# Softmax attention beside a gated FFN: key tiles in blocks of three and two instead of steps of two, a fifth score bank, one accumulator, and the FFN's matmul pairs spread by a planned table

## The chip, the cores and the metric

One core of a Trainium2 chip runs the whole program. The metric is the device time of one execution in microseconds (us). Three executions of the kernel before took 1433.26 to 1434.07 us, 1433.64 us in the median. One further execution was profiled. Its trace has the time of each instruction on TensorE (PE, with its weight loads as PEld), VectorE (DVE), ScalarE (ACT), GpSimd (POOL) and the DMA queues.

## What is computed

The inputs are x of 2048 tokens by 512, the attention weights, and the FFN's three weights with an inner width of 1792. The attention has 32 heads of 16.

```python
def _A_ref(x, wqkv, wo):
    H = 32; Dh = D // H
    qkv = (lambda x, *d: x.transpose(*d))((x @ wqkv).reshape(B, S, 3, H, Dh), 2, 0, 3, 1, 4)
    q, k, v = qkv[0], qkv[1], qkv[2]
    scale = Dh ** -0.5
    scores = jnp.einsum("bhqd,bhkd->bhqk", q, k) * scale
    p = _softmax(scores, axis=-1)
    o = jnp.einsum("bhqk,bhkd->bhqd", p, v)
    return (lambda x, *d: x.transpose(*d))(o, 0, 2, 1, 3).reshape(B, S, D) @ wo

def _B_ref(x, w_gate, w_up, w_down):
    g = _silu(x @ w_gate)
    u = x @ w_up
    return (g * u) @ w_down

x = A_x
xn = _layernorm(x, axis=-1)
s = _A_ref(xn, A_wqkv, A_wo)
g = _silu(_B_ref(xn, B_w_gate, B_w_up, B_w_down))
return x + s * g
```

## The kernel before

A prologue of some 157 us makes the layer norm, the projections to queries, keys and values, and the first FFN tile. Queries and keys go through memory as high and low parts, so that a score matmul has 50 rows (NROW): three products of parts with 16 rows each, and two rows for a shift.

Then one long loop holds the attention. It runs over 32 units: 8 groups of four heads by 4 blocks of 512 queries. A unit goes over 16 key tiles of 128 keys, two tiles to a step (kp), so 8 steps a unit and 256 in all. For a key tile there are two pairs of score matmuls (L826), one pair for each j. The two matmuls of a pair work side by side on the upper and lower half of the array's rows and write the two banks of score[j]. ScalarE then makes one exponential over both banks, 128x1024, into a buffer pr (L828). The value matmuls of a step (L357) are issued one step later, by values(prev) after the next step's first key tile. The four heads stand side by side in the array's columns and add into a bank acc[u % 2]. The trace shows each of them as two matmuls, so that a key tile has two groups of four. When a unit is through, finish, called from the list after one step later, lets VectorE transpose acc[u % 2], divide by the sums and store.

Between the attention's matmuls stand those of the FFN, and at the end those of the output projection. They come as pairs (L175): a matmul into bankx from the upper half of the rows, one into banky from the lower half. ffn and project_out are generators that yield after each pair, and fill(n) takes the next n pairs. A gate and up tile has 24 pairs. When its last pair is issued, ScalarE makes a tanh from bankx (L204), and VectorE multiplies, then splits the result into hh and the down weights into wd (L167, L168, L145, L146). A down tile has 24 or 18 pairs, and its sum is added into facc or y on VectorE. share() calls fill once a step, after the step's four score pairs, with the next number of shares: a gate tile in three steps of 8, a down tile in two or three, an output tile in one step of 12. FIRST sets how many pairs stand between the score pairs of the first step.

The order on each engine is as the program is written (the schedule is manual). ScalarE and VectorE take their instructions in that order. PSUM's eight banks are four for the scores, bankx, banky, and two for acc. Keys and values of a group of heads lie in rings of five chunks of four tiles (RING), loaded by SyncE's queue; queries in two buffers.

Of the kernel before, what the change touches and what calls it, by code (L numbers as in the profile page):

```python
# [19 lines left out]
P = 128  # L20
# [26 lines left out]
KSLOT = (0, 0, 1)  # L47


@with_exitstack  # L50
def tile_block(ctx: ExitStack, tc: tile.TileContext, x, wqkv, wo, w_gate, w_up, w_down, out):
# [24 lines left out]
    banks = (bankx, banky)  # L76
    acc = [pone.tile([P, 512], F32, name=f"acc{i}") for i in range(2)]
    fx = one.tile([P, 2, DC, TB], F32R, name="fx")
# [272 lines left out]
    def values(item):  # L351
        u, kp, probs = item
        v, a = vst[(u // NB * NB + kp * 2 // CT) % RING], acc[u % 2]
        for i in range(2):
            kt = 2 * kp + i
            for h in range(4):
                mm(a[h * 32:h * 32 + DH + 1], v[:, kt % CT, h * (DH + 1):(h + 1) * (DH + 1)],  # L357
                   probs[2 * i + h // 2][:, h % 2], start=kt == 0, stop=kt == KT - 1, skip_group_check=True)

    def normalise(u, first, last, between=None):  # L360
        g, b = divmod(u, NB)
        n = last - first
        o1 = late.tile([P, TB], F32, tag="o1", name="o1")
        dve.transpose(o1[:, :n], acc[u % 2][:, first:last])
        ov = o1[:, :n].rearrange("p (c d) -> p c d", d=32)
        rl = late.tile([P, TB // 32], F32, tag="rl", name="rl")[:, :n // 32]
        dve.reciprocal(rl, ov[:, :, DH])
        if between:
            between()
        dst = on[b][:, first:last].rearrange("p (c s d) -> p c s d", s=2, d=DH)[:, :, g % 2]  # L370
        dve.tensor_mul(dst, ov[:, :, :DH], rl[:, :, None].to_broadcast([P, n // 32, DH]))

    def finish(u):
        g, b = divmod(u, NB)
        normalise(u, 0, TB)
        if g % 2:
            o2 = late.tile([P, TB], F32, tag="o2", name="o2")
# [11 lines left out]
    steps = KT // 2  # L389

# [20 lines left out]

    shares = []

    def plan():
        def tile_of(n, parts):
            shares.extend([n // parts] * parts)

        halved = 0  # L420
        for i in range(2 * NB):
            nf = GROUPS[i % 2].stop - GROUPS[i % 2].start
            for f in range(nf - (i == 0)):
                tile_of(3 * DC, 3 if i or f else 2)
            for t in range(NT):
                if nf == FG:
                    halved += HALVED
                    tile_of(3 * nf, 3 - halved // (NB * NT))
                    halved %= NB * NT
                else:  # L430
                    tile_of(3 * nf, 2)
        for _ in range(EARLY):
            tile_of(3 * (DT - 1), 1)
        for _ in range(NB * NT - NT):
            tile_of(3 * DT, 1)
        shares[0] += 2 - sum(FIRST[:3])
        shares[1] -= 2 + FIRST[3]

    def blocked():
        return not queue or queue[0][0] is not None and ready[queue[0][0]] < DT  # L440

    def share():
        if not blocked() and shares:
            fill(shares.pop(0))


    with ExitStack() as pro:
# [3 lines left out]
        p5 = pro.enter_context(tc.tile_pool(name="p5", bufs=2))  # L451
        plast = pro.enter_context(tc.tile_pool(name="plast", bufs=1))
        pps = pro.enter_context(tc.tile_pool(name="pps", bufs=4, space=PSUM))

        xin = facc
# [48 lines left out]
        for _ in range(11):  # L504
            mm(acc[1][:, :P], busy, busy, start=True, stop=True)
        for kind, i in ((load_w, 8), (load_tile, 1), (load_w, 9), (load_w, 10), (load_tile, 2), (load_w, 11),
# [56 lines left out]
        def turn(t):  # L563
            for c in range(DT):
                turn_one(acc[t % 2], t, c)
            return acc[t % 2].rearrange("p (c f) -> p c f", f=P)

# [41 lines left out]
        xf = one.tile([P, DT, P], F32, tag="th", name="xf")  # L609
        for c, to in enumerate((acc[0], bankx, acc[1], banky)):  # L610
            turn_one(to, 0, c)
        for c, to in enumerate((acc[0], bankx, acc[1], banky)):
            if c == 2:
# [39 lines left out]
        def value_tile(b, t):  # L653
# [9 lines left out]
            else:  # L663
                ps = project([(vh[:, c], vl[:, c], c) for c in range(DT)], xh, xl, slice(t * P, (t + 1) * P), order,
                             acc[1] if b == t == NB - 1 else None)
            if b == 0 and t == 1:
# [16 lines left out]
        for b in range(NB):  # L683
# [3 lines left out]
            for n, (make, i) in enumerate(slots):  # L687
# [12 lines left out]
                if not more and n == 2:  # L700
                    split_gu(0)
                    for bank in acc:
                        dve.memset(bank, 0.0)
                if not more and n in (1, 3):
# [51 lines left out]
        with tc.If(fast < 1):  # L756
            with tc.tile_pool(name="gen", bufs=1) as gen:
                for h in range(2):
                    pool.memset(qst[0][h * HALF:h * HALF + 2].bitcast(F32), 0.0)
                for g in range(NG):  # L760
                    for b in range(NB):
# [14 lines left out]
                        dve.tensor_scalar(mn, mn, -1.0, None, op0=ALU.mult)  # L776
                        top = acc[0][:4 * NT, :P]
                        nc.tensor.transpose(top, mn, ident)
# [28 lines left out]
    split_hidden()  # L807
    plan()
    prev = None

    exps = []
    for u in range(units):
        g, b = divmod(u, NB)
        q = qst[u % 2]
        for kp in range(steps):
            now = u * steps + kp
            probs = []
            for i in range(2):
                kt = 2 * kp + i
                k, kc = kst[(g * NB + kt // CT) % RING], kt % CT  # L820
                if now == i == 0:
                    fill(FIRST[0])
                for j in range(2):
                    for h in range(2):
                        r = slice(h * HALF, h * HALF + NROW)
                        mm(score[j][:, h], k[r, j, kc * P:(kc + 1) * P], q[r, j], start=True, stop=True)  # L826
                    pr = ppool.tile([P, 2, TB], F32, tag="pr", name="pr")
                    exps.append(act(pr, score[j], AF.Exp, scale=0.25))  # L828
# [32 lines left out]
    lo = one.tile([P, D], F32R, tag="th", name="rl")  # L861
    outs = (score[0][:, 0], score[1][:, 0], acc[units % 2], banky)
    half = TB // 2
    cols = [slice(n * half, (n + 1) * half) for n in range(2)]
    spare, *y = [ppool.tile([P, 2, TB], F32, tag="pr", name="y") for _ in range(3)]
    y = [i[:, n] for i in y for n in range(2)]
# [25 lines left out]
    for n in range(2):  # L892
        normalise(units - 1, n * half, (n + 1) * half, partial(low, 0) if n else None)
        turned.append(spare[:, n])
        dve.transpose(turned[n][:, :half], on[NB - 1][:, cols[n]])
# [39 lines left out]
```

## Time and profile before

| | before |
|---|---|
| profiled execution | 1433.38 us |
| its span in the trace | 1431.3 us |
| granted TensorE clock | 1.0 |
| ScalarE, exponentials | 993.1 us in 1024 instructions |
| VectorE busy | 541.9 us |
| DMA | 149.12 MB, mean 104 GB/s |

A row of the timeline gives the start in us, the duration in us, the engine, the line, the instruction with output and inputs, and how many such instructions are merged in the row. A bracket behind it says how long the engine had been idle and what released it. A row of the groups gives busy time and the mean duration in ns of one, then the idle time before them and what ended it. TensorE's matmuls overlap: durations of one (0.39 us for a matmul of a pair) are longer than the distance from one start to the next, and the distance is what a matmul costs in a stream.

### The profile page before, as it was taken

The page shows a single profiled execution, that of the slowest core. Times are in us where ns is not written, and L with a number is a line of the kernel's source. Part 1 is how long each engine was busy: PE and PEld are TensorE (multiplying, and loading weights), DVE is VectorE, ACT ScalarE, POOL GpSimd, SP SyncE. Part 2 cuts the span into 40 slices and gives each one's busy share as a digit, 9 for nine tenths or more (in the row PEclk, how much of TensorE's full clock was granted, in tenths as well). Part 3 has the DMA queues.
Part 4 walks back from the last instruction along what each step waited for, and adds up shares of the span by engine and source line. Part 5 has one row for each costly group of instructions (what it writes and reads, how often), then busy time and mean ns, then how long its engine had stood idle before and what let it go on. Part 6 is the DMA issues. An engine that isn't in the chain of part 4 may idle for free.

```text
span 1431.3 us, 26760 instructions
## 1 busy us (share of the span) xinstructions
PE 1424.6 (100%) x11197; PEld 801.5 (56%) x11197; DVE 541.9 (38%) x901; ACT 1110.0 (78%) x1235; POOL 91.8 (6%) x104
## 2 busy tenths in 40 slices
PE   9999999999999999999999999999999999999998
PEld 7787655555555555555555555555555555555555
DVE  6544443213523443133324341234243422243665
ACT  6733588888888888788888888888888887888764
POOL 4200100000000000000000000000000000000154
PEclk9999999999999999999999999999999999999999
DMA  7878542142264330143543310342724210412552
GB/s 244 262 244 273 136 101 64 24 98 56 71 146 128 84 78 21 40 104 81 111 124 91 96 48 10 79 109 63 168 79 127 59 43 12 101 31 79 196 184 104
DMA packets 127643, 149.12 MB, mean 104 GB/s; under 512 B 12577, under 2 KB 79649, under 8 KB 126750
## 3 DMA queue, kind: packets, MB, share of 16 engines
q1 hardware_dynamic: 122206, 126.72, 34.8%
q0 software_dynamic: 4880, 20.12, 3.8%
q8 instruction: 89, 1.46, 0.5%
q10 hardware_dynamic: 432, 0.52, 0.1%
q14 instruction: 36, 0.29, 0.1%
HBM read 107.46 MB, written 40.11 MB: 103 GB/s over the span
## 4 chain that ended last, share of the span: by engine, by line
PE 89%; DVE 0%; DVEq 0%; issue 0%
PE acc L357 33%; PE bankx L175 32%; PE score L826 20%; PE banky L175 3%; PE acc L873 0%; PE banky L873 0%; PE score L873 0%; DVE y L880 0%; DVE y L886 0%; DVEq L931 0%
## 5 line engine op out<-in xcount | busy, mean ns | idle before, releaser
L828 ACT ACTIVATE pr<-score 128x1024 f32<-128x1024 f32 x1024 | 993.1, 1023 | 222.9 <-PE score L826 222.2
L357 PE MATMUL acc<-pr,vst 128*17 128x512 f32 x4096 | 489.2, 595 | 0.0
L826 PE MATMUL score<-qst,kst 50*128 50x512 f32 x2048 | 352.0, 421 | 0.0
L826 PEld LDWEIGHTS score<-qst,kst 50*128 50x128 f32 x2048 | 177.0, 184 | 263.8 <-ACT pr L828 225.8
L175 PE MATMUL bankx<-fx,guh 64*128 64x512 f32 x896 | 288.6, 392 | 0.1
L175 PE MATMUL banky<-fx,guh 64*128 64x512 f32 x896 | 288.6, 392 | 0.0
L357 PEld LDWEIGHTS acc<-pr,vst 128*17 128x17 f32 x4096 | 93.9, 96 | 234.4 <-issue 233.6
L205 DVE SCALAR_TENSOR_TENSOR ga<-th,bankx 128x512 f32<-128x512 f32 x56 | 38.5, 688 | 450.3 <-ACT th L204 450.3
L175 PEld LDWEIGHTS bankx<-fx,guh 64*128 64x128 f32 x896 | 165.7, 185 | 34.5 <-DVEq L756 0.6
L175 PE MATMUL bankx<-fx,gul 64*128 64x512 f32 x448 | 175.4, 391 | 0.0
L175 PE MATMUL banky<-fx,gul 64*128 64x512 f32 x448 | 175.4, 391 | 0.0
L175 PEld LDWEIGHTS banky<-fx,guh 64*128 64x128 f32 x896 | 165.7, 185 | 2.8
L175 PE MATMUL banky<-wd,hh 64*128 64x512 f32 x672 | 166.8, 389 | 0.0
L175 PE MATMUL bankx<-wd,hh 64*128 64x512 f32 x672 | 166.8, 389 | 0.0
L175 PEld LDWEIGHTS bankx<-wd,hh 64*128 64x128 f32 x672 | 124.0, 185 | 27.2
L175 PEld LDWEIGHTS banky<-wd,hh 64*128 64x128 f32 x672 | 124.0, 185 | 0.7
L175 PEld LDWEIGHTS bankx<-fx,gul 64*128 64x128 f32 x448 | 82.9, 185 | 17.7
L175 PEld LDWEIGHTS banky<-fx,gul 64*128 64x128 f32 x448 | 82.8, 185 | 1.6
L593 PE MATMUL ps<-xt,wh 128*128 128x512 f32 x256 | 80.9, 396 | 0.1
L223 DVE COPY facc<-bankx 128x512 f32<-128x512 f32 x16 | 11.1, 692 | 171.5 <-PE banky L175 171.5
L136 DVE TENSOR_TENSOR gul<-gur,guh 128x1024 fp32r<-128x1024 f32 x56 | 68.6, 1225 | 2.1
L380 POOL DMA_DIRECT2D o_d<-o x12 | 6.5, 542 | 757.2 <-DVE o L378 757.2
(160 smaller groups left out, 1063.5 us busy)
## 6 DMA issues: line engine op xcount, KB each, us to landing
gur<-in_B_w_gate_dram SPq DMA_DIRECT2D x56, 256.0 KB
gur<-in_B_w_up_dram SPq DMA_DIRECT2D x56, 256.0 KB
wdr<-in_B_w_down_dram SPq DMA_DIRECT2D x56, 256.0 KB
kst<-k_d SPq DMA_DIRECT2D x192, 64.0 KB
qst<-q_d SPq DMA_DIRECT2D x192, 64.0 KB
fx<-xt_d SPq DMA_DIRECT2D x24, 512.0 KB
q_d<-parts SPq DMA_DIRECT2D x16, 512.0 KB
k_d<-parts SPq DMA_DIRECT2D x16, 512.0 KB
```

What stands on the lines that cost most here:

```text
L136: dve.tensor_sub(lo, raw, hi.bitcast(F32))
L175: mm(bank, lhs[h], rhs[h], start=start, stop=stop)
L205: dve.scalar_tensor_tensor(ga, th, 1.0, bankx, op0=ALU.add, op1=ALU.mult)
L223: dve.tensor_copy(facc[:, t], bankx)
L357: mm(a[h * 32:h * 32 + DH + 1], v[:, kt % CT, h * (DH + 1):(h + 1) * (DH + 1)], probs[2 * i + h // 2][:, h % 2], start=kt == 0, stop=kt == ...
L380: (pool if g < NG - 1 else sp).dma_start(o_d[g // 2, b], o2)
L593: mm(ps, w, a[:, c], start=n == 0, stop=n == 3 * DT - 1)
L826: mm(score[j][:, h], k[r, j, kc * P:(kc + 1) * P], q[r, j], start=True, stop=True)
L828: exps.append(act(pr, score[j], AF.Exp, scale=0.25))
```

## The change

A unit's 16 key tiles are now taken in six blocks, four of three tiles and two of two (SIZES), so there are 192 blocks instead of 256 steps. The block's first two score pairs, those of its first tile, stand together as before; then come the values of the block before, and finish where that block ended a unit. The other score pairs stand alone, and after each of them fill takes a share of the FFN's pairs: four shares in a block of three, two in a block of two.

The block's last score pair writes its second matmul into a bank of its own, spare, and its exponential is made as two of 128x512, one from score[1] and one from spare. The bank for this comes from the accumulator, which is now one bank, acc, for all units. The exponentials have eight buffers instead of six. The rings have four chunks instead of five, and the next group's keys and values are loaded when the last unit of a group has done with the values of a chunk.

plan() chooses before the program is built, by dynamic programming over the FFN's tiles, in which order each unit's blocks of three and two stand and how many pairs each block takes. It aims at four pairs to a tile of keys, with at least 12 in a block of three and 6 in a block of two, and no block crosses an FFN tile's border. What it chose:

| key tiles in the block | FFN pairs in the block | blocks | pairs behind the last score pair |
|---|---|---|---|
| 3 | 12 | 94 | 3 |
| 3 | 14 | 1 | 3 |
| 3 | 16 | 31 | 4 |
| 3 | 9 | 2 | 2 |
| 2 | 6 | 17 | 3 |
| 2 | 8 | 43 | 4 |
| 2 | 12 | 4 | 6 |

Units 7 and 8, as an example: (2, 6) (3, 12) (2, 6) (3, 12) (3, 12) (3, 12), then (3, 12) (3, 12) (3, 12) (2, 8) (3, 16) (2, 8).

TensorE's order before, early in the loop, around one step's value matmuls. The names are those of the code; x8 merges the eight value matmuls of two key tiles, and 17x512 is the shape of one output.

```order
L175 MATMUL bankx<-fx,guh 128x512
L175 MATMUL banky<-fx,guh 128x512
L826 MATMUL score_8961<-qst_8975,kst_8963 128x512 x2
L826 MATMUL score_8962<-qst_8975,kst_8963 128x512 x2
L357 MATMUL acc_87<-pr,vst_8964 17x512 x8
L826 MATMUL score_8961<-qst_8975,kst_8963 128x512 x2
L826 MATMUL score_8962<-qst_8975,kst_8963 128x512 x2
L175 MATMUL bankx<-fx,guh 128x512
L175 MATMUL banky<-fx,guh 128x512
L175 MATMUL bankx<-fx,gul 128x512
L175 MATMUL banky<-fx,gul 128x512
```

The same place in the changed program, a block of three after a block of three:

```order
L871 MATMUL score_8965<-qst_8975,kst_548 128x512 x2
L871 MATMUL score_8966<-qst_8975,kst_548 128x512 x2
L416 MATMUL acc<-pr,vst_549 17x512 x12
L871 MATMUL score_8965<-qst_8975,kst_552 128x512 x2
L235 MATMUL bankx<-fx,guh 128x512
L235 MATMUL banky<-fx,guh 128x512
L235 MATMUL bankx<-fx,guh 128x512
L235 MATMUL banky<-fx,guh 128x512
L235 MATMUL bankx<-fx,gul 128x512
L235 MATMUL banky<-fx,gul 128x512
L871 MATMUL score_8966<-qst_8975,kst_552 128x512 x2
L235 MATMUL bankx<-fx,guh 128x512
```

The value matmuls come twelve at a time instead of eight, and the second tile's two score pairs, which stood together, now have three FFN pairs between them. The end of that block on TensorE:

```order
L235 MATMUL banky<-fx,guh 128x512
L235 MATMUL bankx<-fx,gul 128x512
L235 MATMUL banky<-fx,gul 128x512
L871 MATMUL score_8966<-qst_8975,kst_552 128x512
L871 MATMUL spare<-qst_8975,kst_552 128x512
L235 MATMUL bankx<-fx,guh 128x512
L235 MATMUL banky<-fx,guh 128x512
L235 MATMUL bankx<-fx,guh 128x512
L235 MATMUL banky<-fx,guh 128x512
```

The last score pair's second matmul goes to spare. On ScalarE, two steps before (the tanh of a gate tile stands among the exponentials):

```order
L828 ACTIVATE pr<-score_8961 128x1024
L828 ACTIVATE pr<-score_8962 128x1024
L828 ACTIVATE pr<-score_8961 128x1024
L828 ACTIVATE pr<-score_8962 128x1024
L204 ACTIVATE th<-bankx 128x512
L828 ACTIVATE pr<-score_8961 128x1024
L828 ACTIVATE pr<-score_8962 128x1024
L828 ACTIVATE pr<-score_8961 128x1024
L828 ACTIVATE pr<-score_8962 128x1024
```

and the changed program, a block of two and the beginning of the next:

```order
L264 ACTIVATE th<-bankx 128x512
L874 ACTIVATE pr<-score_8965 128x1024
L874 ACTIVATE pr<-score_8966 128x1024
L874 ACTIVATE pr<-score_8965 128x1024
L876 ACTIVATE pr<-score_8966 128x512
L877 ACTIVATE pr<-spare 128x512
L874 ACTIVATE pr<-score_8965 128x1024
L874 ACTIVATE pr<-score_8966 128x1024
```

The block's last exponential has become two halves, and the gate's tanh stands behind a block's halves.

The core of the diff (most of plan, the renamed banks of the prologue and of the tail left out):

```diff
-RING = NB + 1
+RING = NB
...
-FIRST = (4, 5, 2, 2)
-HALVED = 2
+SIZES = {2: 2, 3: 4}
+FIRST = (4, 0, 4, 3, 3, 2, 2)
...
+    least, most = {2: 6, 3: 12}, {2: 12, 3: 16}
...
+                        c = cost + 100 * max(0, least[k] - n) + abs(n - 4 * k)
...
+    for k, n in blocks:
+        m = 2 * k - 2
+        parts.append((k, [0, 0] + [n // m + (i < n % m) for i in range(m)]))
+    parts[0] = 3, list(FIRST[1:])
+    return parts
...
-        u, kp, probs = item
-        v, a = vst[(u // NB * NB + kp * 2 // CT) % RING], acc[u % 2]
-        for i in range(2):
-            kt = 2 * kp + i
+        u, tiles, probs = item
+        for i, kt in enumerate(tiles):
+            v = vst[(u // NB * NB + kt // CT) % RING]
             for h in range(4):
-                mm(a[h * 32:h * 32 + DH + 1], v[:, kt % CT, h * (DH + 1):(h + 1) * (DH + 1)],
+                mm(acc[h * 32:h * 32 + DH + 1], v[:, kt % CT, h * (DH + 1):(h + 1) * (DH + 1)],
                    probs[2 * i + h // 2][:, h % 2], start=kt == 0, stop=kt == KT - 1, skip_group_check=True)
...
-        dve.transpose(o1[:, :n], acc[u % 2][:, first:last])
+        dve.transpose(o1[:, :n], acc[:, first:last])
...
-    ppool = ctx.enter_context(tc.tile_pool(name="ppool", bufs=6))
+    ppool = ctx.enter_context(tc.tile_pool(name="ppool", bufs=8))
...
+    spare = spool.tile([P, 512], F32, name="spare")
...
-        for kp in range(steps):
-            now = u * steps + kp
+        kt = 0
+        for i in range(steps):
+            now = u * steps + i
+            size, parts = blocks[now]
+            tiles = range(kt, kt + size)
+            kt += size
             probs = []
-            for i in range(2):
-                kt = 2 * kp + i
-                k, kc = kst[(g * NB + kt // CT) % RING], kt % CT
-                if now == i == 0:
-                    fill(FIRST[0])
-                for j in range(2):
-                    for h in range(2):
-                        r = slice(h * HALF, h * HALF + NROW)
-                        mm(score[j][:, h], k[r, j, kc * P:(kc + 1) * P], q[r, j], start=True, stop=True)
-                    pr = ppool.tile([P, 2, TB], F32, tag="pr", name="pr")
-                    exps.append(act(pr, score[j], AF.Exp, scale=0.25))
-                    if i == 0 and j == 1 and now:
-                        tc.add_manual_dep(exps[-1].ins, exps[-3].ins.name, settled, reason="order of the slots' writes")
-                    probs.append(pr)
-                    if now == i == 0 and j:
-                        fill(FIRST[1])
-                    elif (now, i, j) in ((0, 1, 0), (1, 0, 0)):
-                        fill(FIRST[2 + now])
-                if i == 0:
+            if not now:
+                fill(FIRST[0])
+            for n in range(2 * size):
+                t, j = tiles[n // 2], n % 2
+                if n == 2:
                     catch_up()
-                if i == 0 and prev:
-                    values(prev)
-            old, prev = prev, (u, kp, probs)
-            share()
-            if old and old[1] == steps - 1:
-                after.append(partial(finish, old[0]))
-            if kp == 0:
-                if u + 1 < units:
-                    load_q(u + 1)
-                    load_shift(u + 1)
-            if g + 1 < NG and (b == 0 and kp == 0 or b == NB - 1 and kp in (2, 4, 6)):
-                load_k(g + 1, kp // 2)
-                load_v(g + 1, kp // 2)
+                    if prev:
+                        values(prev)
+                        if prev[1][-1] == KT - 1:
+                            finish(prev[0])
+                k, kc = kst[(g * NB + t // CT) % RING], t % CT
+
+                room, whole = score[j], n < 2 * size - 1
+                for h in range(2):
+                    r = slice(h * HALF, h * HALF + NROW)
+                    mm(room[:, h] if whole or not h else spare, k[r, j, kc * P:(kc + 1) * P], q[r, j], start=True, stop=True)
+                pr = ppool.tile([P, 2, TB], F32, tag="pr", name="pr")
+                if whole:
+                    made = act(pr, room, AF.Exp, scale=0.25)
+                else:
+                    act(pr[:, 0], room[:, 0], AF.Exp, scale=0.25)
+                    made = act(pr[:, 1], spare, AF.Exp, scale=0.25)
+                exps.append(made)
+                if n == 1 and now:
+                    tc.add_manual_dep(exps[-1].ins, exps[-3].ins.name, settled, reason="order of the slots' writes")
+                probs.append(pr)
+                fill(parts[n])
+            if prev and prev[0] // NB + 1 < NG and prev[0] % NB == NB - 1:
+                done = prev[1][-1] + 1
+                while len(coming) < done // CT:
+                    load_k(prev[0] // NB + 1, len(coming))
+                    load_v(prev[0] // NB + 1, len(coming))
+                    coming.append(now)
+                if done == KT:
+                    coming.clear()
+            prev = u, tiles, probs
+            if i == 0 and u + 1 < units:
+                load_q(u + 1)
+                load_shift(u + 1)
```

More of the change, by code (lines that the diff above doesn't have):

```diff
@@ L47, with plan @@
 KSLOT = (0, 0, 1)
+def plan():
+    sizes = sorted(SIZES)
+    least, most = {2: 6, 3: 12}, {2: 12, 3: 16}
+    left = []
+    for i in range(2 * NB):
+        nf = GROUPS[i % 2].stop - GROUPS[i % 2].start
+        left += [3 * DC] * nf + [3 * nf] * NT
+    left = left[2:]
+    blocks = [(3, sum(FIRST)), (2, 3 * DC - sum(FIRST))]
+    rest = [3 * (DT - 1)] * EARLY + [3 * DT] * (NT * (NB - 1))
+    ends = H // 4 * NB * sum(SIZES.values()) - len(rest)
+    whole = tuple(SIZES[k] for k in sizes)
+    start = tuple(SIZES[k] - sum(b[0] == k for b in blocks) for k in sizes)
+    layers = [{(0, left[0], start): (0, None)}]
+    for _ in range(len(blocks), ends):
+        new = {}
+        for state, (cost, _) in layers[-1].items():
+            tile_no, rem, kinds = state
+            kinds = kinds if any(kinds) else whole
+            for i, k in enumerate(sizes):
+                if not kinds[i]:
+                    continue
+                for n in range(least[2] // 2, min(most[k], rem) + 1):
+                    if n == rem:
+                        after = tile_no + 1, left[tile_no + 1] if tile_no + 1 < len(left) else 0
+                    elif rem - n >= least[2] // 2:
+                        after = tile_no, rem - n
+                    else:
+                        continue
+                    if after[0] < len(left) or len(layers) + len(blocks) == ends:
+                        key = after + (kinds[:i] + (kinds[i] - 1,) + kinds[i + 1:],)
+                        c = cost + 100 * max(0, least[k] - n) + abs(n - 4 * k)
+                        if key not in new or c < new[key][0]:
+                            new[key] = c, (state, k, n)
+        layers.append(new)
+    state = min((v[0], s) for s, v in layers[-1].items() if s[0] == len(left))[1]
+    kinds = state[2]
+    middle = []
+    for layer in layers[:0:-1]:
+        state, k, n = layer[state][1]
+        middle.append((k, n))
+    blocks += middle[::-1]
+    order = []
+    while len(order) < len(rest):
+        order += [k for i, k in reversed(list(enumerate(sizes))) for _ in range(kinds[i])]
+        kinds = whole
+    blocks += zip(order, rest)
+    parts = []
+    for k, n in blocks:
[3 more added lines that the diff above has]
+    return parts
 @with_exitstack
@@ L76, in tile_block @@
     banks = (bankx, banky)
-    acc = [pone.tile([P, 512], F32, name=f"acc{i}") for i in range(2)]
+    acc = pone.tile([P, 512], F32, name="acc")
     fx = one.tile([P, 2, DC, TB], F32R, name="fx")
@@ L376, in finish @@
         if g % 2:
-            o2 = late.tile([P, TB], F32, tag="o2", name="o2")
+            o2 = late.tile([P, TB], F32, tag="o1", name="o2")
             dve.transpose(o2, on[b])
@@ L388, in tile_block @@
     units = NG * NB
-    steps = KT // 2
+    steps = sum(SIZES.values())
     u0 = units - NB + 1
@@ L410, in fill @@
             given += 1
[L414 to L437, printed above, removed]
+    blocks = plan()
     def blocked():
         return not queue or queue[0][0] is not None and ready[queue[0][0]] < DT
-    def share():
-        if not blocked() and shares:
-            fill(shares.pop(0))
     with ExitStack() as pro:
@@ L452, in tile_block @@
         plast = pro.enter_context(tc.tile_pool(name="plast", bufs=1))
+        pex = pro.enter_context(tc.tile_pool(name="pex", bufs=1, space=PSUM))
         pps = pro.enter_context(tc.tile_pool(name="pps", bufs=4, space=PSUM))
+        extra = pex.tile([P, 512], F32, name="extra")
+        turns = acc, extra
         xin = facc
@@ L504, in tile_block @@
         for _ in range(11):
-            mm(acc[1][:, :P], busy, busy, start=True, stop=True)
+            mm(extra[:, :P], busy, busy, start=True, stop=True)
         for kind, i in ((load_w, 8), (load_tile, 1), (load_w, 9), (load_w, 10), (load_tile, 2), (load_w, 11),
@@ L609, in tile_block @@
         xf = one.tile([P, DT, P], F32, tag="th", name="xf")
-        for c, to in enumerate((acc[0], bankx, acc[1], banky)):
+        for c, to in enumerate((acc, bankx, extra, banky)):
             turn_one(to, 0, c)
-        for c, to in enumerate((acc[0], bankx, acc[1], banky)):
+        for c, to in enumerate((acc, bankx, extra, banky)):
             if c == 2:
@@ L701, in tile_block @@
                     split_gu(0)
-                    for bank in acc:
-                        dve.memset(bank, 0.0)
+                    dve.memset(acc, 0.0)
                 if not more and n in (1, 3):
@@ L861, in tile_block @@
     lo = one.tile([P, D], F32R, tag="th", name="rl")
-    outs = (score[0][:, 0], score[1][:, 0], acc[units % 2], banky)
+    outs = (score[0][:, 0], score[1][:, 0], spare, banky)
     half = TB // 2
     cols = [slice(n * half, (n + 1) * half) for n in range(2)]
-    spare, *y = [ppool.tile([P, 2, TB], F32, tag="pr", name="y") for _ in range(3)]
+    room, *y = [ppool.tile([P, 2, TB], F32, tag="pr", name="y") for _ in range(3)]
     y = [i[:, n] for i in y for n in range(2)]
```

13 lines of the change are left out of this document (7 added, 6 removed).

## The prediction

> **What bounds the kernel now.** I read the page's shares first, then the chain that ended last, then single steps of the timeline. The page:
>
> ```profile
> span 1431.3 us, 26760 instructions
> PE 1424.6 (100%) x11197; PEld 801.5 (56%) x11197; DVE 541.9 (38%) x901; ACT 1110.0 (78%) x1235; POOL 91.8 (6%) x104
> ...
> PE 89%; DVE 0%; DVEq 0%; issue 0%
> ...
> L828 ACT ACTIVATE pr<-score 128x1024 f32<-128x1024 f32 x1024 | 993.1, 1023 | 222.9 <-PE score L826 222.2
> ```
>
> TensorE is busy for the whole span and the chain runs along it. ScalarE is second at 78%, and its 222.9 us of idle time before the exponentials ended with a score pair: ScalarE waits for TensorE, not the other way. So only what shortens TensorE's stream counts. But "busy" hides bubbles, since matmuls overlap; they show in the distance from start to start. One step's visit to the value matmuls, from the timeline of TensorE in narrow windows (start in us, duration, instruction, count):
>
> ```profile
> 707.49 0.40 PE L826 MATMUL score<-qst,kst 50*128 50x512 f32 x2
> 707.72 0.40 PE L826 MATMUL score<-qst,kst 50*128 50x512 f32 x2
> 708.04 0.62 PE L357 MATMUL acc<-pr,vst 128*17 128x512 f32 x4
> 708.49 0.61 PE L357 MATMUL acc<-pr,vst 128*17 128x512 f32 x4
> 708.91 0.61 PE L357 MATMUL acc<-pr,vst 128*17 128x512 f32 x4
> 709.34 0.61 PE L357 MATMUL acc<-pr,vst 128*17 128x512 f32 x4
> 709.88 0.49 PE L826 MATMUL score<-qst,kst 50*128 50x512 f32 x2
> 710.22 0.40 PE L826 MATMUL score<-qst,kst 50*128 50x512 f32 x2
> 710.45 0.40 PE L175 MATMUL bankx<-wd,hh 64*128 64x512 f32 x1
> 710.69 0.39 PE L175 MATMUL bankx<-wd,hh 64*128 64x512 f32 x1
> ```
>
> A pair of score matmuls, and a pair of FFN matmuls, takes 0.23 us when its like or the other stands before it (707.49 to 707.72, 710.22 to 710.45 to 710.69). Four value matmuls side by side take 0.43 us, two such groups to a key tile; the step from the first tile's groups to the second's (708.49 to 708.91) costs nothing more. But 707.72 to 710.22 is 2.50 us, and two score pairs and four groups make only 0.46 + 1.72 = 2.18. **A visit to the value matmuls costs 0.32 us besides its work**: about 0.1 going in, 0.1 coming out, 0.1 on the first score pair, whose duration is 0.49 instead of 0.40. There are 256 visits.
>
> **The change, part by part.**
>
> *Fewer visits.* 32 units of six blocks are 192 visits instead of 256. All score, value and FFN matmuls stay. 64 x 0.32 = **20.5 us** less on TensorE, all of it on the path.
>
> *Score pairs spread between FFN pairs.* This alternates score and FFN about four times a block instead of once. Whether that costs, and what a late release costs, the first step shows, where such singles stand already (PEld is the weight load, which carries the wait):
>
> ```profile
> 157.91 1.03 ACT L828 ACTIVATE pr<-score 128x1024 f32<-128x1024 f32 x1 [1.04 <-PE score L826]
> 158.78 0.40 PE L175 MATMUL bankx<-fx,gul 64*128 64x512 f32 x1
> 158.99 0.19 PEld L826 LDWEIGHTS score<-qst,kst 50*128 50x128 f32 x2 [0.21 <-ACT pr L828]
> 159.02 0.47 PE L826 MATMUL score<-qst,kst 50*128 50x512 f32 x2
> 159.33 0.39 PE L175 MATMUL bankx<-fx,guh 64*128 64x512 f32 x1
> 159.74 1.03 ACT L828 ACTIVATE pr<-score 128x1024 f32<-128x1024 f32 x1
> 159.90 0.51 PE L826 MATMUL score<-qst,kst 50*128 50x512 f32 x2
> 160.24 0.40 PE L175 MATMUL bankx<-fx,gul 64*128 64x512 f32 x1
> 160.71 0.40 PE L175 MATMUL bankx<-fx,guh 64*128 64x512 f32 x1
> 160.82 0.19 PEld L826 LDWEIGHTS score<-qst,kst 50*128 50x128 f32 x2
> 160.94 0.41 PE L826 MATMUL score<-qst,kst 50*128 50x512 f32 x2
> 161.18 0.39 PE L175 MATMUL bankx<-fx,gul 64*128 64x512 f32 x1
> ```
>
> A single score pair between FFN pairs keeps the step (160.71, 160.94, 161.18): alternating costs nothing. A score pair's weights are loaded 0.05 us after the exponential that frees its banks ends (159.74 + 1.03 = 160.77, load 160.82). With 0.12 us between that load and the pair's turn (160.94) nothing is lost; with 0.02 (load 158.99, turn 158.78 + 0.23 = 159.01) the next pair comes 0.31 after instead of 0.23, so 0.08 is lost; a pair that stands still loses its wait and 0.11 more (159.90 to 160.24).
>
> *The halved last exponential.* ScalarE gets 192 instructions more. What they take is read from a gate's tanh, which also reads 128x512 from PSUM, with exponentials behind it:
>
> ```profile
> 326.24 0.60 ACT L204 ACTIVATE th<-bankx 128x512 f32<-128x512 f32 x1
> 326.74 1.94 ACT L828 ACTIVATE pr<-score 128x1024 f32<-128x1024 f32 x2
> 327.64 1.03 ACT L828 ACTIVATE pr<-score 128x1024 f32<-128x1024 f32 x1
> ...
> 707.92 1.94 ACT L828 ACTIVATE pr<-score 128x1024 f32<-128x1024 f32 x2 [0.58 <-PE score L826]
> ```
>
> Half an exponential ends 0.60 after its start and holds ScalarE 0.50; a whole one ends after 1.02 and holds it 0.90 to 0.92 (326.74 to 327.64; 1.94 - 1.02). Two halves hold it 0.08 longer than one whole: 192 x 0.08 = 15 us, which TensorE's work covers, as a block of three with 12 FFN pairs is 18 x 0.23 + 6 x 0.43 + 0.32 = 7.0 us long after another three, or 6.2 after a two, and holds ScalarE 5 x 0.92 + 1.00 = 5.6. Inside the block, score pairs with three FFN pairs behind each come every 4 x 0.23 = 0.93 us and exponentials every 0.92: just in step. An exponential starts 0.43 after its pair (707.49, 707.92). The tight place is the next block's second score pair, which needs the first half read out: the block's last pair at 0, first half 0.43 to 1.03, weights 1.08; the pair's turn after three FFN pairs and a score pair is 5 x 0.232 = 1.16. The lead of 0.08 lies between the two cases above; on the line through them it costs 0.03. That holds for 94 blocks (3 tiles, 12 pairs), 17 (2, 6) and 1 (3, 14): 112 x 0.03 = **3.4 us** more. Its bounds are 0 and the 0.11 of a restart, 12.3 us. The 78 blocks with four or more FFN pairs behind the last score pair have a lead of 0.31 or more. Two late blocks of (3, 9) have two pairs behind most scores: 0.70 against 0.92, three waits of about 0.2 each with their restarts: **1.4 us** for both.
>
> On the Trainium skill's "ScalarE: Activation LUTs", section "What ACT_TABLE_LOAD costs": an ACTIVATE with immediate scale and bias takes 186 ns plus 0.833 ns an element, and two back to back overlap by 93 ns, so splitting speaks against itself; by it a half is 0.61 and a whole holds the engine 0.95, which is more than the pairs' 0.93. As an estimate from that page the first half would end 0.07 later and the sum be about 7 us higher. This trace shows 0.60 and 0.90 to 0.92, and the sum goes by it.
>
> *Gate tiles' ends.* Now a tanh falls between a step's last exponential and the next step's first, and pushes the second score bank's release late:
>
> ```profile
> 328.72 0.19 PEld L826 LDWEIGHTS score<-qst,kst 50*128 50x128 f32 x2
> 328.78 0.45 PE L826 MATMUL score<-qst,kst 50*128 50x512 f32 x2
> 329.07 0.39 PE L175 MATMUL bankx<-fx,guh 64*128 64x512 f32 x1
> ...
> L204 ACT ACTIVATE th<-bankx 128x512 f32<-128x512 f32 x55 | 32.9, 598 | 8.0 <-PE banky L175 1.7 <-PE bankx L175 0.2
> ```
>
> Weights load 0.05 after the exponential of 327.64 ends at 328.67, and the next pair comes 0.29 later instead of 0.23. With 55 gate tiles in the loop that is at most 3 us. Afterwards that score pair stands behind three or four FFN pairs, 0.7 us and more later, so the wait goes: **2 us** less (bounds 0 and 3).
>
> *One accumulator.* The next unit's first value matmul must wait for VectorE's transpose of acc, where it now has the other bank. VectorE at a gate's end, and the transpose and load rows:
>
> ```profile
> 326.05 0.39 PE L826 MATMUL score<-qst,kst 50*128 50x512 f32 x2
> 329.91 0.69 DVE L146 TENSOR_TENSOR wd<-wdr,wd 128x512 fp32r<-128x512 f32 x1
> 711.02 0.71 DVE L364 STREAM_TRANSPOSE o<-acc 128x512 f32<-128x512 f32 x1
> ...
> 702.51 8.48 SPq L101 DMA_DIRECT2D qst<-q_d  x4
> ```
>
> VectorE is through with the tile 4.55 us after the new step's first score pair (326.05 to 330.60), the transpose ends at 5.3. The gate ends that fall on a unit's end are all followed by a block (3, 12) after a three, whose successor's visit begins 7.0 + 0.55 = 7.6 us after that pair: 2.3 us to spare. Cost 0; without the cover it would be at most 31 waits.
>
> *Ring of four.* A group's first keys and values now load when the last unit has done with their values, in its third block, some 16 us into its 38 us (the loop's 1250 us by 32 units), and are needed at the next unit's start. 22 us cover a load of 8.5 us (the row of qst above). Cost 0. Eight exponential buffers for six, the shorter first block, and the last block's halves: 0, within half a microsecond either way.
>
> **Sum**, against the profiled execution's 1433.4 us (2.1 above its span, and 0.3 below the median): 1433.4 - 20.5 - 2 + 3.4 + 1.4 = 1415.7, so **1416 us**.
>
> **The rivals.**
>
> *The releases come later than the lead allows.* If the exponentials fall 0.1 us behind in the (3, 12) blocks, each of the 112 tight places costs 0.13 instead of 0.03, and the time is 1427. For it speaks that 0.93 against 0.92 leaves no slack to catch up; against it, that exponentials in an unbroken row come at 0.90 (326.74, 327.64) and that blocks begin with an idle ScalarE.
>
> *Slower: halves cost like wholes.* Were the first half to end 1.02 after its start, the 112 places would wait 0.42 - 0.08 and restart at 0.11, 0.45 each, and the 78 others 0.42 - 0.31 + 0.11 = 0.22: 50 + 17 us, 1433.4 - 22.5 + 67 + 1.4 = 1479. It decides from 0.19 us a tight place on, that is with the half ending 0.16 later than the tanh. Against it stand 55 tanh rows at 598 ns.
>
> *The visit's price is not fixed* but goes with its work: nothing saved, 1436 with the other terms. Against it: the groups inside are at an even 0.43 across the border of two key tiles.
>
> *The new waits bite* (acc or keys): 0.6 us at 31 unit ends, 1435. The spare 2.3 and 13 us speak against it.
>
> **How the numbers follow.** Forecast (1411 to 1421) 0.62; late releases (1421 to 1431) 0.18; better than forecast, with no lead lost (1408 to 1411), 0.06; fixed price wrong or new waits 0.07; slower 0.07. The range 1408 to 1427 takes in both bounds of the unknowns: 64 x 0.34 + 3 off and nothing added gives 1408.6; 20.5 off with 12.3 + 1.4 added gives 1427. About 0.2% (2.9 us) is what a measurement can tell from no change; with it faster 0.87, the same 0.06, slower 0.07.
>
> **What would show it.** Right: 192 visits, each still 0.32 beside its groups; single score pairs at 0.23; the second score pair of a block after (3, 12) with durations a little over 0.40 and the next value group a few hundredths late; ScalarE's idle time before exponentials smaller by some 30 us. Wrong: second score pairs that start at the half's end with durations of 0.50, weight loads that wait for ScalarE at a hundred places, halves longer than 0.60, a first value matmul of a unit behind VectorE, or TensorE idle before a key load.

## The result and the profile after

The changed kernel takes **1419.83 us** (median of four, 1419.49 to 1420.0), the kernel before 1433.76 (four, 1433.26 to 1434.07) beside it. The ratio is 0.9903 with a 95% interval of 0.9886 to 0.992, so it is faster by about 1%. That lies inside the range of the prediction, 3.8 us above its 1416. The profiled execution took 1419.49 with a span of 1417.7 and a granted clock of 0.999.

The page of the changed kernel: the shares, the chain that ended last, and the groups of the exponentials and of the value matmuls.

```profile
span 1417.7 us, 26890 instructions
PE 1409.6 (99%) x11197; PEld 817.8 (58%) x11197; DVE 543.2 (38%) x900; ACT 1112.7 (78%) x1427; POOL 90.2 (6%) x102
...
PE 88%; DVE 1%; ACT 0%; issue 0%; DVEq 0%
...
L874 ACT ACTIVATE pr<-score 128x1024 f32<-128x1024 f32 x832 | 816.7, 1033 | 201.8 <-PE score L871 190.0
L416 PE MATMUL acc<-pr,vst 128*17 128x512 f32 x4096 | 476.8, 594 | 0.6 <-DVE o L423 0.6
...
L876 ACT ACTIVATE pr<-score 128x512 f32<-128x512 f32 x192 | 114.8, 598 | 11.9 <-PE spare L871 1.8
L877 ACT ACTIVATE pr<-spare 128x512 f32<-128x512 f32 x192 | 114.1, 595 | 0.0
```

TensorE is still the bound, with the same 11197 matmuls. The halves take 598 and 595 ns, as the gate's tanh did. ScalarE's idle time before exponentials went from 222.9 to 201.8 + 11.9 = 213.7 us, 9 less, where the prediction looked for some 30. ScalarE's busy time as a whole rose by 2.7 us. And 0.6 us before the value matmuls are new: TensorE waited for VectorE's transpose of acc.

One visit to the value matmuls, between a block of three and the next (rows of TensorE, its weight load and ScalarE out of the timeline):

```profile
703.93 0.60 ACT L876 ACTIVATE pr<-score 128x512 f32<-128x512 f32 x1
...
704.44 0.40 PE L871 MATMUL score<-qst,kst 50*128 50x512 f32 x2
704.58 0.18 PEld L871 LDWEIGHTS score<-qst,kst 50*128 50x128 f32 x2 [0.19 <-ACT pr L876]
704.67 0.41 PE L871 MATMUL score<-qst,kst 50*128 50x512 f32 x2
705.01 0.62 PE L416 MATMUL acc<-pr,vst 128*17 128x512 f32 x4
705.45 0.61 PE L416 MATMUL acc<-pr,vst 128*17 128x512 f32 x4
...
707.17 0.61 PE L416 MATMUL acc<-pr,vst 128*17 128x512 f32 x4
707.71 0.50 PE L871 MATMUL score<-qst,kst 50*128 50x512 f32 x2
708.05 0.40 PE L235 MATMUL bankx<-wd,hh 64*128 64x512 f32 x1
708.29 0.39 PE L235 MATMUL bankx<-wd,hh 64*128 64x512 f32 x1
```

From the second score pair (704.67) to the first FFN pair (708.05) are 3.38 us, and its work is two score pairs (0.46) and six groups of four value matmuls (2.58): 0.34 beside the work, of which 0.32 is the fixed price and 0.02 the late half. The late half is seen in the weight load: the first half ends at 704.53, the weights load at 704.58, 0.09 before the pair's turn. How often that happens stands in the view of the waits (engine and tile, releaser: us in total, times, longest):

```profile
PEld score L871 <- ACT pr L874: 153.5, 186, 0.9
...
PEld score L871 <- ACT pr L876: 19.9, 104, 0.3
```

The weight load, not TensorE, waited 104 times for a first half; the prediction counted 112 tight places.

### The profile page after: what moved, and what is told of

Its sections match the earlier page's. It is cut to its first block, busy times and chain, and to the rows that moved or that the text cites. A ratio compares the mean times of both kernels' runs of the same rounds, so it can differ in the third digit from the quotient of the medians.

```text
span 1417.7 us, 26890 instructions
## 1 busy us (share of the span) xinstructions
PE 1409.6 (99%) x11197; PEld 817.8 (58%) x11197; DVE 543.2 (38%) x900; ACT 1112.7 (78%) x1427; POOL 90.2 (6%) x102
## 4 chain that ended last, share of the span: by engine, by line
PE 88%; DVE 1%; ACT 0%; issue 0%; DVEq 0%
PE acc L416 32%; PE bankx L235 31%; PE score L871 19%; PE banky L235 5%; PE spare L871 0%; ACT pr L874 0%; PE banky L917 0%; PE score L917 0%; DVE facc L408 0%; DVE o L423 0%; PE spare L917 0%; DVE y L924 0%; DVE y L389 0%; DVE facc L407 0%; DVE y L240 0%
## 5 line engine op out<-in xcount | busy, mean ns | idle before, releaser
L874 ACT ACTIVATE pr<-score 128x1024 f32<-128x1024 f32 x832 | 816.7, 1033 | 201.8 <-PE score L871 190.0
L416 PE MATMUL acc<-pr,vst 128*17 128x512 f32 x4096 | 476.8, 594 | 0.6 <-DVE o L423 0.6
L871 PE MATMUL score<-qst,kst 50*128 50x512 f32 x1856 | 398.2, 418 | 0.0
L871 PEld LDWEIGHTS score<-qst,kst 50*128 50x128 f32 x1856 | 192.9, 184 | 216.4 <-ACT pr L874 153.5
L416 PEld LDWEIGHTS acc<-pr,vst 128*17 128x17 f32 x4096 | 100.5, 97 | 256.4 <-issue 254.5
L235 PE MATMUL banky<-wd,hh 64*128 64x512 f32 x672 | 189.3, 392 | 0.0
L235 PE MATMUL bankx<-wd,hh 64*128 64x512 f32 x672 | 189.3, 392 | 0.0
L265 DVE SCALAR_TENSOR_TENSOR ga<-th,bankx 128x512 f32<-128x512 f32 x56 | 38.5, 688 | 371.8 <-ACT th L264 371.8
L876 ACT ACTIVATE pr<-score 128x512 f32<-128x512 f32 x192 | 114.8, 598 | 11.9 <-PE spare L871 1.8
L877 ACT ACTIVATE pr<-spare 128x512 f32<-128x512 f32 x192 | 114.1, 595 | 0.0
L871 PE MATMUL spare<-qst,kst 50*128 50x512 f32 x192 | 75.7, 394 | 0.0
```

Of the source, the lines that this page charges most:

```text
L235: mm(bank, lhs[h], rhs[h], start=start, stop=stop)
L265: dve.scalar_tensor_tensor(ga, th, 1.0, bankx, op0=ALU.add, op1=ALU.mult)
L416: mm(acc[h * 32:h * 32 + DH + 1], v[:, kt % CT, h * (DH + 1):(h + 1) * (DH + 1)], probs[2 * i + h // 2][:, h % 2], start=kt == 0, stop=kt ...
L871: mm(room[:, h] if whole or not h else spare, k[r, j, kc * P:(kc + 1) * P], q[r, j], start=True, stop=True)
L874: made = act(pr, room, AF.Exp, scale=0.25)
L876: act(pr[:, 0], room[:, 0], AF.Exp, scale=0.25)
```

## Experiments

The kernels were run on three chips, each group beside the kernel before: the first four with 1433.73 us for before (13 runs), the next two with 1433.42 (nine), the last with 1433.86 (nine). Distances in the text are from start to start of TensorE's rows, averaged over the loop, from its first score pair to its last group of value matmuls.

**The changed kernel again (c0_after)**, unedited, beside the kernels of the first group.

> The changed kernel once more, as the measure for the runs beside it on the same chip. 1419.8 us, 14 below the kernel before.

Measured: 1419.86 (1419.65 to 1420.02), ratio 0.9903 (0.9886 to 0.992), the same again.

**The end of the program (e1_gate_rest_early).** The end of the changed kernel is 1.9 us longer than that of before: from the last group of value matmuls to the end of the span 14.55 us against 12.69. Rows of the timeline, first before, then after:

```profile
1417.34 1.91 PE L357 MATMUL acc<-pr,vst 128*17 128x512 f32 x16
...
1419.32 0.45 DVE L364 STREAM_TRANSPOSE o<-acc 128x256 f32<-128x256 f32 x1 [0.32 <-PE acc L357]
```

```profile
1401.85 1.91 PE L416 MATMUL acc<-pr,vst 128*17 128x512 f32 x16
1403.43 0.68 DVE L407 SCALAR_TENSOR_TENSOR facc<-facc,hh 128x512 f32<-128x512 f32 x1
1404.15 1.67 DVE L408 TENSOR_TENSOR facc<-facc,on 128x512 f32<-128x512 f32 x1
1405.74 0.43 DVE L423 STREAM_TRANSPOSE o<-acc 128x256 f32<-128x256 f32 x1
```

The DVE L364 or L423 row is the first transpose of the last unit's sums. Before, it starts 1.98 after the last value matmuls begin, released by them (the bracket). After, it starts 3.89 behind them and waits for no matmul: VectorE still does the two passes of gate_rest. Their place is set by a count from the beginning of the last unit, its fifth and sixth step. A unit had eight steps and now has six blocks, so the sixth is the last. The line that counts is not in the diff. The edit lets them come two blocks sooner:

```diff
-            if 0 <= now - (units - 1) * steps - 4 < EARLY:
-                gate_rest(now - (units - 1) * steps - 4)
+            if 0 <= now - (units - 1) * steps - 2 < EARLY:
+                gate_rest(now - (units - 1) * steps - 2)
```

> gate_rest, two VectorE passes for each of two token tiles, is moved from blocks 4 and 5 of the last unit to blocks 2 and 3. Theory: in the changed kernel the second of them stands in the unit's last block (six blocks where there were eight steps), and VectorE is at it until 1405.8 us while the last value matmul ended at 1403.8, so that the last transpose comes 2 us late; moved, the time falls by 1.9 us against the changed kernel, and the span from the last value matmuls to the end is 12.7 us as before the change, not 14.6. Rival: the tail is bound by TensorE's last products and the stores, then 0.3 us or less.

Measured: 1418.18 (1418.02 to 1418.29), ratio 0.9891 (0.9875 to 0.9908), 1.7 us below the changed kernel on the same chip. The loop takes 1246.3 us, against 1246.1, and the end 12.82. Its timeline:

```profile
1402.21 1.91 PE L416 MATMUL acc<-pr,vst 128*17 128x512 f32 x16
1403.18 0.69 DVE L390 SCALAR_TENSOR_TENSOR y<-banky,y 128x512 f32<-128x512 f32 x1
1404.24 0.45 DVE L423 STREAM_TRANSPOSE o<-acc 128x256 f32<-128x256 f32 x1 [0.37 <-PE acc L416]
```

The transpose is released by the matmuls again, 2.03 after they begin. So this part of the lost gain is shown.

**Blocks of two alone (e3_twos_only).** All of the change (halves, one accumulator, ring of four, spread score pairs) without the fewer visits:

```diff
-SIZES = {2: 2, 3: 4}
-FIRST = (4, 0, 4, 3, 3, 2, 2)
+SIZES = {2: 8}
+FIRST = (4, 0, 4, 4, 4)
...
-    blocks = [(3, sum(FIRST)), (2, 3 * DC - sum(FIRST))]
+    blocks = [(2, sum(FIRST)), (2, 3 * DC - sum(FIRST))]
...
-    parts[0] = 3, list(FIRST[1:])
+    parts[0] = 2, list(FIRST[1:])
```

> All units in eight blocks of two tiles, 256 visits to the value matmuls, everything else as in the changed kernel (halves, one accumulator, ring of four, spread FFN pairs). Theory, a fixed price of 0.32 us a visit: 20.5 us more for 64 visits, 3 less since nearly all blocks have four pairs behind the last score pair, 1.9 less since gate_rest falls on the fifth and sixth of eight blocks: 1435 us. Rival, the gain came from the spreading and the halves: 1420 to 1423 us.

Measured: 1437.16 (1436.36 to 1437.97), ratio 1.0022 (1.0013 to 1.0032): without its larger blocks the change costs some 3 us. The distances into, in and out of the visits hold 85.7 us above the pace of the work for 255 visits, against 65.4 for 191 in the changed kernel: 20.3 us for 64 visits, 0.317 each. Both sums hold other waits too: here 2.7 us at four single visits, there 3.3 of late halves and one wait. Without them a visit costs **0.326 us** here and 0.325 there.

Single waits of TensorE, 3.8 us in all, more than make up the 2 us over the expectation. Two are at the only accumulator, which VectorE was still reading out, in the waits and in the timeline:

```profile
PE acc L416 <- DVE o L423: 1.2, 2, 1.0
PEld acc L416 <- DVE o L423: 4.6, 9, 1.4
...
1333.58 0.69 DVE L303 TENSOR_TENSOR fx<-wor,fx 128x512 fp32r<-128x512 f32 x1
1334.19 0.71 DVE L423 STREAM_TRANSPOSE o<-acc 128x512 f32<-128x512 f32 x1
1334.95 1.91 PE L416 MATMUL acc<-pr,vst 128*17 128x512 f32 x16 [0.97 <-DVE o L423]
```

They made the distance to the values 1.05 and 0.31 longer, both late in the loop, where VectorE also splits the output projection's operands. The weight load is shown as waiting nine times, but in the other seven cases the distance to the values is the usual 0.327. In them the transpose ends 0.17 before the values; in most units 2.1 are to spare. Two other places cost more than the accumulator: 1.8 at 1382, where VectorE still reads the banks of an output tile (L389, L390), and 0.7 at 169, at the first FFN tile's end (L265, L266).

**The spread alone, in the kernel before (e4_before_spread).** Half of a step's FFN pairs go between the second key tile's two score pairs. Blocks, accumulators and whole exponentials stay.

```diff
+                    if i == 1 and j == 0:
+                        rest = 0 if blocked() or not shares else shares.pop(0)
+                        fill(rest // 2)
...
-            share()
+            fill(rest - rest // 2)
```

> The kernel before, with half of a step's FFN pairs moved between the second key tile's two score pairs. Theory, each score pair put into a run of FFN pairs costs 0.008 us, as the first pairs of a run come at 0.234 and later ones at 0.231: 256 x 0.008 = 2 us more, and about 1.5 to 2 us less since a gate tile's tanh no longer makes the next score pair late: 1433.5 us, with FFN pairs at 0.2327 on the mean instead of 0.2317. Rival, the slower FFN pairs of the changed kernel have another cause (the clock, its halves): FFN pairs stay at 0.2317 and the time is 1432 us.

Measured: 1480.39 (1479.93 to 1480.85), ratio 1.0324 (1.0307 to 1.0342). The expected time was missed by 47 us, as a cost in it had been left out. The timeline shows it:

```profile
703.61 0.40 PE L826 MATMUL score<-qst,kst 50*128 50x512 f32 x2
704.05 1.03 ACT L828 ACTIVATE pr<-score 128x1024 f32<-128x1024 f32 x1
704.78 0.40 PE L826 MATMUL score<-qst,kst 50*128 50x512 f32 x2
705.12 0.19 PEld L826 LDWEIGHTS score<-qst,kst 50*128 50x128 f32 x2 [0.39 <-ACT pr L828]
705.12 0.50 PE L826 MATMUL score<-qst,kst 50*128 50x512 f32 x2
705.56 0.62 PE L357 MATMUL acc<-pr,vst 128*17 128x512 f32 x4
```

The step's last score pair (703.61) now has only half of the FFN pairs behind it. Its whole exponential ends at 705.08, and the next step's second pair, whose turn was 704.78 + 0.23 = 705.01, starts with its weight load at 705.12. On the mean the distance between the two score pairs is 0.10 longer and that to the values 0.08: 256 x 0.18 = 46 us. What it was made for still shows: the distance between FFN pairs is 232.9 ns on the mean of 1636 (231.7 before), so breaking the run of FFN pairs does cost a little.

**Whole last exponentials (e2_no_halves)** in the changed kernel, spare unused:

```diff
-                room, whole = score[j], n < 2 * size - 1
+                room, whole = score[j], True
```

> The changed kernel with the block's last exponential whole again: both its matmuls go to score[1], one 128x1024 exponential, spare unused. Theory: the next block's second score pair must then wait for an exponential that ends 0.42 us later. With three FFN pairs behind the last score pair the lead of 0.08 turns into a wait of 0.34 and a restart of 0.11; with four it is 0.42 - 0.31 + 0.11 = 0.22, as the kernel before showed with its pairs spread (47 us for 256 steps, 0.18 each). 112 x 0.42 + 78 x 0.2 = 63 us more than the changed kernel: 1480 us. Rival: ScalarE catches up in the next visit and TensorE's later work absorbs it: below 1440 us.

Measured: 1485.87 (1485.71 to 1485.94), ratio 1.0364 (1.0348 to 1.0379); 66 us above the changed kernel. A block's border:

```profile
701.35 0.39 PE L871 MATMUL score<-qst,kst 50*128 50x512 f32 x2
701.78 1.02 ACT L874 ACTIVATE pr<-score 128x1024 f32<-128x1024 f32 x1
702.27 0.40 PE L871 MATMUL score<-qst,kst 50*128 50x512 f32 x2
702.86 0.19 PEld L871 LDWEIGHTS score<-qst,kst 50*128 50x128 f32 x2 [0.63 <-ACT pr L874]
702.86 0.50 PE L871 MATMUL score<-qst,kst 50*128 50x512 f32 x2 [0.19 <-ACT pr L874]
703.29 0.62 PE L416 MATMUL acc<-pr,vst 128*17 128x512 f32 x4
```

The second pair comes 0.59 after the first instead of 0.23, as its exponential ends at 702.80, and the values follow after 0.43 instead of 0.33: 0.46 at this place. That is the prediction's slower rival: it named 0.45 a tight place and 67 us. So the bank spare, and the accumulator given up for it, carry the change. Without them it would have lost 52 us instead of gaining 14.

**Blocks of four (e5_fours).** If the visit's price is fixed, fewer and larger visits go on paying. A planner of its own chooses blocks of two, three and four tiles, with 0.32 for each visit, 0.25 for each FFN pair short of three behind a single score pair, and 0.03 for a tight block:

```diff
+    most = {2: 12, 3: 18, 4: 24}
...
+                    lack = 6 * (k - 1) - n
+                    c = cost + 0.32 + 0.25 * max(0, lack) + 0.03 * (lack <= 0 and n < 8 * (k - 1))
...
+    blocks = [(3, 20)] + blocks[::-1]
...
-            if 0 <= now - (units - 1) * steps - 4 < EARLY:
-                gate_rest(now - (units - 1) * steps - 4)
+            if 0 <= now - starts[units - 1] - 2 < EARLY:
+                gate_rest(now - starts[units - 1] - 2)
```

It makes 166 blocks, 76 of them (4, 18), 65 (2, 6), 10 (3, 12) and 8 (4, 24).

> A plan that may also take four key tiles to a block and any number of blocks to a unit: 166 blocks (76 of (4, 18), 65 of (2, 6), 10 of (3, 12), 8 of (4, 24), the rest single ones), and gate_rest early. Theory: 26 visits fewer at 0.32 are 8.3 us, the early gate_rest 1.8, against 52 more single score pairs at 0.008 and 39 more tight places at 0.03: 1419.8 - 8.3 - 1.8 + 0.4 + 1.2 = 1411 us. Rival: after a block of four ScalarE has no free exponential buffer (eight in all) until the first values are read, and the score pairs wait for it: each block after a four costs 0.2 or more, 84 x 0.2 = 17 us, and the time is 1425 or more.

Measured: 1409.78 (1409.32 to 1411.88), ratio 0.9832 (0.9819 to 0.9846). In the view of the waits, ScalarE now stands for a free exponential buffer:

```profile
ACT pr L865 <- PE acc L402: 74.2, 84, 1.4
```

A block of four and the next block's first tile hold ten exponentials, and there are eight buffers. The 74 us cost TensorE nothing that shows in the time: it is 1.2 below the expectation, and the rival that priced them gave 1425 or more. The profiled execution, the slowest of the five, has one stall at the loop's start, in the timeline:

```profile
167.13 0.50 PE L862 MATMUL score<-qst,kst 50*128 50x512 f32 x2
...
168.03 0.68 DVE L251 SCALAR_TENSOR_TENSOR ga<-th,bankx 128x512 f32<-128x512 f32 x1
168.76 0.49 PE L221 MATMUL bankx<-fx,guh 64*128 64x512 f32 x1 [1.14 <-DVE ga L251]
```

The first FFN tile ends inside the first block there, and VectorE, late from the preparation, holds its banks.

**Blocks of four with the changed kernel's start (e6_fours_start):**

```diff
-FIRST = (4, 0, 4, 4, 4, 4, 4)
+FIRST = (4, 0, 4, 3, 3, 2, 2)
...
-    blocks = [(3, 20)] + blocks[::-1]
+    blocks = [(3, 18), (2, 6)] + blocks[::-1]
```

> As e5_fours, but with the first two blocks as in the changed kernel, (3, 18) and (2, 6). In e5_fours the first FFN tile ends already in the first block, when VectorE is still held up behind the freed prologue's buffers, and TensorE loses 1.3 + 0.6 + 0.2 + 0.2 + 0.2 + 0.1 = 2.6 us there (a score pair at 167.13 that is followed only at 168.76, and the pairs up to 173.4). Theory: that goes, 1407 to 1408 us. Rival: the prologue's buffers come free at their own time and the same wait shows a block later: 1409 us or more.

Measured: 1409.1 (1408.73 to 1410.64), ratio 0.9829 (0.9816 to 0.9842), 0.7 below e5_fours where two to three were expected, and less than the spread of either. The stall is gone from the trace. But four of e5_fours' five executions ran 1.5 to 2.6 us faster than its profiled one, so they can hardly have had all of the stall; what it costs in most executions stays open. This is the fastest kernel of the study, 24.8 us below before on the same chip (1433.86) and 10.8 below the changed one, which ran on another chip (1419.86).

## Why the prediction was right, and what it left out

The terms of its sum beside what the two traces hold. The spans differ by 1417.7 - 1431.3 = -13.6 us. The measured terms are sums of the distances between TensorE's starts, each against the pace of its kind.

| step of the prediction | predicted, us | measured, us |
|---|---|---|
| fewer visits | -20.5 | -20.9 |
| gate tiles' ends | -2 | -2.4 |
| halved last exponential, tight places | +3.4 | +2.4 |
| two blocks (3, 9) | +1.4 | +1.4 |
| score pairs spread between FFN pairs | 0 | +3.5 |
| one accumulator | 0 | +0.6 |
| start of the loop; end of the program | 0, within 0.5 | +0.1; +1.9 |
| sum | -17.7 | -13.4 |

The terms leave 0.2 us of the difference unexplained.

*Fewer visits: right.* In the kernel before, a visit has on the mean 95 ns more on the way in, 12 on the first group, 113 on the way out and 106 behind the first score pair: 0.326, and 64 of them 20.9. Blocks of two alone (e3_twos_only) keep that price, and blocks of four went on gaining. The rival of a price that goes with the work is false. The Trainium skill's "TensorEngine Tiling (Array Packing)", section "Key Properties", says that a change of the tiling mode drains TensorE. It fits the trace in that 95 and 113 ns more stand at the two borders between matmuls on 64 rows and those on 32 columns; a drain as such is not shown, and the price of 0.32 stands only in the trace.

*Tight places: right in place and near in size.* The distance from the second score pair to the values is 338.9 ns on the mean of 187 visits, against 326.2 of 254 before: 2.4 us. (The first block, the two (3, 9) and the one wait for the accumulator are counted in their own rows.) The late releases of the first rival did not come, and what decides is the half's 0.60 us, as e2_no_halves shows.

*The two (3, 9) blocks: right.* The weight loads of three score pairs wait for ScalarE in turn (the rows are below, with the accumulator's), and each of the two blocks loses 0.69, with 0.1 of it in the distance to the values.

*Gate tiles' ends: right.* The 55 long distances from a score pair to an FFN pair that followed a gate's tanh, 2.4 us in all before, are gone.

*Spread score pairs: the step that was mis-sized.* "Alternating costs nothing" was read from a few rows, to 0.01 us. Over the whole loop an FFN pair behind an FFN pair comes after 233.3 ns on the mean of 1509, against 231.7 of 1891 before, and one behind a score pair after 234.3 against 231.9: 1509 x 1.6 + 450 x 2.4 = 3.5 us. The rise is the same in kind in e3_twos_only (233.0 without four distances that hold a wait for VectorE), e6_fours_start (233.4) and, with nothing else of the change, in e4_before_spread (232.9). Over half of it is that a run's first distance, 234.3 already before where the others had 231.3, now comes 641 times instead of 259: by that alone the mean would be 232.6. That the spread raises it is shown; why it does in TensorE is not.

*The start of the loop and the end of the program: not in the sum.* The loop starts 0.3 us earlier, but its first block loses 1.0 in waits for exponentials, where the first step lost 0.5. FIRST leaves two FFN pairs behind that block's last score pair, not the three of the plan's table, so it waits as the (3, 9) blocks do. For the end "within half a microsecond" fell, since gate_rest's due time counts blocks. With e1_gate_rest_early 1.7 of the 1.9 us come back.

*One accumulator: nearly right.* It cost one wait, in the changed kernel's timeline (with the first of the two (3, 9) blocks below it):

```profile
1288.16 0.69 DVE L303 TENSOR_TENSOR fx<-wor,fx 128x512 fp32r<-128x512 f32 x1
1288.77 0.71 DVE L423 STREAM_TRANSPOSE o<-acc 128x512 f32<-128x512 f32 x1
1289.54 1.05 PE L416 MATMUL acc<-pr,vst 128*17 128x512 f32 x8 [0.55 <-DVE o L423]
...
1312.49 0.18 PEld L871 LDWEIGHTS score<-qst,kst 50*128 50x128 f32 x1 [0.39 <-ACT pr L874]
1313.40 0.19 PEld L871 LDWEIGHTS score<-qst,kst 50*128 50x128 f32 x2 [0.38 <-ACT pr L874]
1313.89 0.19 PEld L871 LDWEIGHTS score<-qst,kst 50*128 50x128 f32 x2 [0.30 <-ACT pr L876]
```

What held VectorE there is the splitting of the output projection's weights, not a gate's end, and the block behind is a (2, 6), whose visit comes soon. The prediction had looked at gates alone.

*ScalarE's idle time: the check failed.* It took the time saved on TensorE and the 15 us of the halves' extra hold off the idle time before exponentials. That group counts only what stands directly before an exponential, and it fell by 9. The time itself did not hang on it.

So the four priced steps gave 19.5 us where 17.7 were expected, and what the sum held for nothing or for small took 6.1 back. That the first error covers a part of the second is luck: without it the sum would have missed by six instead of four.

## What to carry to other kernels

A fixed price for changing over between two kinds of matmul is worth measuring from start to start, and then larger visits pay, here up to four key tiles and past the point where ScalarE runs out of buffers; but the bank that is read last before each border must come free soon enough, or the border costs more than the visit. When a loop's count of steps changes, look through every line that counts in steps, above all the ones that the diff leaves alone. A cost of 1 or 2 ns for a pair of matmuls isn't seen in ten rows but is microseconds over two thousand: take the mean over the loop.

## What the runs showed of the hardware that was not expected

FFN pairs aren't evenly spaced behind a score pair. In the changed kernel the first distance between two of them is 235.3 ns on the mean, the second 231.3, the third 233.2; in the kernel before 234.3, 231.4 and 234.1, and about 231 from the fifth on.

VectorE's addition L408 took 1.67 us in the end of the changed kernel, where the pass L407 of the same size took 0.68. GpSimd ran two tensor operations of 1.62 us each from 1403.65 on, beside it; in the kernel before the same addition (L348) stood beside GpSimd's and took 1.66. The changed kernel's trace has the comparison: the addition L323, of the same size, took 0.69 in all ten rows of the loop with no GpSimd operation beside it, and 1.66 to 1.69 in all five with one of GpSimd's additions beside it. Two of these rows, and the GpSimd addition beside the second:

```profile
1333.15 0.69 DVE L323 TENSOR_TENSOR wd<-wd 128x512 fp32r<-128x512 f32 x1
1336.90 1.38 POOL L374 TENSOR_TENSOR y<-y,hh 128x512 f32<-128x512 f32 x1 [3.19 <-DVE y L390]
1337.18 1.66 DVE L323 TENSOR_TENSOR wd<-wd 128x512 fp32r<-128x512 f32 x1
```

So what runs beside it makes the difference, and not only the kind of operation. L407 began before GpSimd's addition and kept its 0.68. A GpSimd memset beside the same kind of addition (L206 at 165.08) left it at 0.69.

ScalarE may wait for buffers 84 times, 74 us in all, without a cost that shows in the time (e5_fours); a weight load that comes 0.1 us too late, at most of the 256 steps, cost 47 us in e4_before_spread.
